# Moving three VectorE operations on a table ahead of two evacuations, in a Fourier-filter and feed-forward kernel

## The chip, the cores and the metric

One core of one Trainium2 chip. The metric is the device time of one execution in microseconds (us), the median of the runs of a kernel. Before the change it was 792.48 us (three runs, 791.69 to 793.87).

Names: TensorE is PE in the profile (its weight loads PEld), VectorE is DVE, ScalarE is ACT, GpSimd is POOL; SP only issues transfers. L291 is line 291 of the kernel's file. The change adds two lines above most of the code, so L443 of before is L445 of after.

## The reference, cut to what matters

```python
def _attn_ref(x, filt_r, filt_i):            # x: (8, 3008, 256), filters: (1505, 256)
    X = np.fft.rfft(x, axis=1)
    Y = X * (filt_r + 1j * filt_i)[None, :, :]
    return np.fft.irfft(Y, n=x.shape[1], axis=1)

def _moe_ref(x, w_in, w_out, beta):          # 24064 tokens, 256 -> 2048 -> 256
    h = x @ w_in
    return (h * (1.0 / (1.0 + np.exp(-beta * h)))) @ w_out
```

The kernel does the Fourier transforms as products with tables of sines and cosines, in two stages each way (3008 = 47 x 64). It makes the tables itself while the first of the eight batches is loading. From about 43 us on it is a steady stream of matmuls of the feed-forward part, with the later batches' filtering woven in.

## The kernel before

Only the set-up, the first 43 us, matters. The order in the source is the order of each engine's queue.

The angles of the second table are made in two halves of 12 x 64 columns: the first half on VectorE, the second on GpSimd.

```python
def angles(h, eng):
    ...
    eng.tensor_tensor(u[:], ka[...], kb[...], ALU.add)                     # L264
    eng.tensor_scalar(r[:], u[:], ROUND_C, ROUND_C, ALU.add, ALU.subtract) # L270: rounding
    eng.tensor_tensor(u[:], u[:], r[:], ALU.subtract)                      # L271
...
angles(0, nc.vector)
angles(1, gp)
```

ScalarE makes two of the table's five parts from the angles. The other three are a negated copy and two plain copies on VectorE:

```python
def t2_more(h, eng):
    ks_ = slice(h * NH, (h + 1) * NH)
    nc.vector.tensor_scalar_mul(t2[:, ks_, 4, :], t2[:, ks_, 1, :], -1.0)  # L290
    eng.tensor_copy(t2[:, ks_, 3, :], t2[:, ks_, 2, :])                    # L291
    eng.tensor_copy(t2[:, ks_, 0, :], t2[:, ks_, 1, :])                    # L292
```

The first stage of the first batch runs in eight units, each two PSUM tiles that are evacuated by VectorE (False) or ScalarE (True). `warm` puts dummy matmuls on TensorE.

```python
for i in range(2):
    first1(i, (True, True))
    warm(2 if i == 0 else 8)
t2_part(0, 0)                       # ScalarE
first1(2, (False, False))
warm(2)
for part in (1, 2):
    t2_part(0, part)                # ScalarE
...
for i in range(3, 5):
    first1(i, (False, False))
    warm(2)
t2_more(0, nc.vector)
first1(5, (True, True))
warm(2)
first1(6, (True, True))
warm(1)
first1(7, (False, True))
tabs = [table3(0, 0, ...), table3(0, 2, ...)]   # transposes of the table, L352
```

Then follow twelve products with the filter on VectorE, each two operations (L443). Products 1 to 3 read the first group of filter rows, 4 to 6 the second, 7 to 12 the third.

```python
for dst, ps in zip((p_t, q_t), pss):
    nc.vector.tensor_tensor(dst[:], ps[:], fri[:, 2 * i : 2 * i + 2, :], ALU.mult)
```

GpSimd's queue issues the loads of the feed-forward weights and of the second batch. They stand behind a small copy that reads the second filter group and so waits for it:

```python
for p0 in (H, M + H):
    gp.tensor_copy(held[p0 : p0 + H], fri[p0 : p0 + H, 2 * KG - 1, :1])
...
load_win(0)
load_win(1)
load_wout(0)
...                                  # second batch, the rest of the output weights
```

After the products: GpSimd scales the output weights as they land, SP's queue loads filter rows for the second batch, and one long VectorE operation ends the set-up.

```python
for i in range(4):
    scale_wout(i)                    # GpSimd, L149
for at in (0, M):
    for go in load_filter(frr, filt_r, at, 0, JG, nc.sync):
        go()
...
nc.vector.tensor_scalar_mul(t3[M:P], t3b[M:P], -1.0)      # L586, 64x3072
```

## Time and profile before

| before | us | view |
|---|---|---|
| span of the profiled execution | 789.8 | page |
| TensorE busy | 776.7 (98%) | page, part 1 |
| last table copy ends, table's transposes start | 16.52, 16.66 | timeline |
| first product, seventh product start | 18.89, 27.98 | timeline |
| last piece of the third filter group lands | 27.80 | times of landings |
| first product with the output weights (end of set-up) | 43.13 | timeline |

In a timeline line the columns are start, duration, engine, line, operation, out<-in, shape, count and, in brackets, idle time of the engine and what is thought to have ended it. This is VectorE's timeline before, 10 to 17 us:

```profile
10.58 2.88 DVE L107 CAST a_t<-psa 128x384 bf16<-128x384 f32 x6 [1.75 <-PE psa L326]
13.38 0.35 DVE L290 TENSOR_SCALAR t<-t 128x768 bf16<-128x768 bf16 x1
13.64 0.98 DVE L291 COPY t<-t 128x768 bf16<-128x768 bf16 x1
14.55 1.97 DVE L292 COPY t<-t 128x768 bf16<-128x768 bf16 x1
```

And GpSimd's, of the same time:

```profile
10.05 1.46 POOL L264 TENSOR_TENSOR u<-ka,kb 128x768 f32<-128x768 f32 x1
11.60 2.81 POOL L270 TENSOR_SCALAR r<-u 128x768 f32<-128x768 f32 x1
14.49 1.80 POOL L271 TENSOR_TENSOR u<-u,r 128x768 f32<-128x768 f32 x1
16.25 0.32 POOL L307 CAST id_f<-ident 16x16 f32<-16x16 bf16 x1
```

The three operations have the same shape. One took 0.35 us, one 0.98, one 1.97, and the two long ones end 0.2 us after a GpSimd operation: 14.41 and 16.29. TensorE waits for the last of them. The profile's bracket names another cause:

```profile
16.66 0.83 PE L352 MATMUL pt<-ident,t 128*128 128x128 bf16 x12 [2.28 <-POOL id_f L307]
```

The program waits there for VectorE's two table copies (the multiply stands ahead of them in the queue) and for an identity matrix that GpSimd had made by 5.7 us. GpSimd's L307 only happened to end at the same time. The wait of 2.28 us is VectorE's copy.

Further down, the seventh product and the long operation at the end of the set-up, with GpSimd's scaling beside it (VectorE's, VectorE's and GpSimd's timelines):

```profile
27.08 0.68 DVE L443 TENSOR_TENSOR qb_t<-ps2q,fri 128x512 bf16<-128x512 f32 x1
27.98 0.69 DVE L443 TENSOR_TENSOR pb_t<-ps,fri 128x512 bf16<-128x512 f32 x1 [0.22 <-PE pb L396]
```
```profile
40.66 1.49 DVE L586 TENSOR_SCALAR t<-t3b 64x3072 bf16<-64x3072 bf16 x1
```
```profile
39.44 1.89 POOL L149 TENSOR_TENSOR wout_sb<-frr,rbeta_sb 128x1024 bf16<-128x1024 f32 x1 [3.66 <-DMA frr<-in_moe_w_out_dram]
```

The seventh product idled 0.22 us and began 0.18 us after the last filter piece landed. That is the sign of a landing as the true cause, though the bracket says PE.

The DMA is nearly full all through the set-up. The view by stretches gives, for each, its length, the busy time and the instructions of PE, PEld, DVE, ACT and POOL, then the clock granted to TensorE, the DMA's busy share and its rate in GB/s:

```profile
17.00:28.00 11.00, 9.64 (x134) 8.65 (x132) 10.00 (x22) 10.13 (x18) 6.87 (x13) 1.00 1.08 221
28.00:36.30 8.30, 7.76 (x106) 6.73 (x104) 8.17 (x14) 6.77 (x13) 3.47 (x3) 1.00 1.06 252
```

### The profile page before, as it was taken

The numbers are of one execution on the slowest core, as the hardware profiler recorded it, in microseconds if no ns is written. First come the engines' busy times: TensorE is split into PE (matmuls) and PEld (weight loads), VectorE is DVE, ScalarE is ACT, GpSimd is POOL, SyncE is SP. The second block draws the span as 40 slices with busy tenths as digits, with TensorE's granted clock in tenths as the row PEclk, the third lists the DMA queues.
The fourth block names the chain that finished last, engine by engine and source line by source line (L and its number), as shares of the span: only waits on it lengthen the run. The fifth ranks groups of instructions, "written<-read, shape, count | busy, mean of one in ns | idle before, by whom it ended". The sixth has DMA issues, their size and how long they took to land.

```text
span 789.8 us, 15387 instructions
## 1 busy us (share of the span) xinstructions
PE 776.7 (98%) x6104; PEld 547.6 (69%) x6104; DVE 396.3 (50%) x644; ACT 596.9 (76%) x920; POOL 144.6 (18%) x143
## 2 busy tenths in 40 slices
PE   7899999999999999999999999999999999999998
PEld 4767667766777667876678766686667766776665
DVE  7946935755537464465534746367452761500101
ACT  5887886886678866788677876778767788677776
POOL 9322510330013200131002310024000340000000
PEclk9999999999999999999999999999999999999999
DMA  9978687116811178011860228412370214010101
GB/s 187 232 193 213 155 212 218 49 67 187 215 45 47 68 200 218 29 68 70 216 181 28 86 97 199 152 36 88 110 222 27 74 68 127 30 52 28 54 27 53
DMA packets 83380, 91.43 MB, mean 116 GB/s; under 512 B 3759, under 2 KB 73537, under 8 KB 82287
## 3 DMA queue, kind: packets, MB, share of 16 engines
q1 hardware_dynamic: 80204, 73.95, 30.5%
q0 software_dynamic: 2816, 16.26, 10.8%
q8 instruction: 47, 0.77, 0.4%
q10 hardware_dynamic: 288, 0.26, 0.1%
q14 instruction: 25, 0.20, 0.1%
HBM read 57.16 MB, written 46.66 MB: 131 GB/s over the span
## 4 chain that ended last, share of the span: by engine, by line
PE 93%; DVE 3%; POOL 2%; issue 1%; ACT 1%; DVEq 0%; ACTq 0%; POOLq 0%
PE acc L840 41%; PE hps L805 40%; PE ps L613 3%; PE ps L536 3%; PE ps L635 2%; PE ps L661 2%; DVE ost L107 1%; PE psz L456 1%; POOL xg L116 0%; POOL r L270 0%; ACT a L105 0%; DVE q_t L650 0%; DVE p_t L646 0%; DVE q_t L647 0%; PE pt L352 0%
## 5 line engine op out<-in xcount | busy, mean ns | idle before, releaser
L814 ACT ACTIVATE gT<-hps,beta_sb 128x512 bf16<-128x512 f32 x752 | 516.8, 687 | 175.3 <-PE hps L805 165.5
L840 PE MATMUL acc<-wout_sb,gT 128*128 128x256 bf16 x3008 | 455.1, 272 | 1.2 <-ACT ost L105 0.2
L805 PE MATMUL hps<-y,win_sb 128*128 128x512 bf16 (+7 forms) x1728 | 447.7, 351 | 0.3 <-DVE y L109 0.3
L840 PEld LDWEIGHTS <-gT 128*128 128x128 bf16 x3008 | 285.3, 98 | 132.7 <-issue 4.7
L805 PEld LDWEIGHTS <-win_sb 128*128 128x128 bf16 x1728 | 164.7, 98 | 24.8 <-issue 0.7
L651 POOL TENSOR_TENSOR v_t<-p_t,q_t 128x512 bf16<-128x512 f32 x84 | 106.7, 1270 | 375.3 <-DVE q_t L650 372.7
L107 DVE COPY ost<-acc 128x512 f32<-128x512 f32 (+1 forms) x88 | 56.2, 677 | 193.6 <-PE acc L840 188.0
L107 DVE CAST a<-ps 96x512 bf16<-96x512 f32 x96 | 65.9, 686 | 85.6 <-PE ps L613 85.6
L109 DVE TENSOR_SCALAR y<-ps 128x376 bf16<-128x376 f32 (+2 forms) x120 | 64.5, 541 | 64.3 <-PE ps L536 64.2
L646 DVE TENSOR_TENSOR p_t<-ps,frr 128x512 f32<-128x512 f32 x84 | 58.1, 691 | 31.8 <-PE ps L635 29.4
L650 DVE TENSOR_TENSOR q_t<-ps,fri 64x512 f32<-64x512 f32 x84 | 58.2, 693 | 1.2
L647 DVE SCALAR_TENSOR_TENSOR q_t<-ps,fri 64x512 f32<-64x512 f32 x84 | 57.4, 684 | 1.1
L536 PEld LDWEIGHTS <-zz 96*128 96x128 bf16 x512 | 35.4, 97 | 29.0
L105 ACT ACTIVATE z<-ps 128x512 bf16<-128x512 f32 x84 | 49.5, 590 | 0.7 <-PE ps L661 0.7
L613 PE MATMUL ps<-xg,t 94*96 94x512 bf16 x112 | 41.9, 381 | 0.2 <-DVE a L107 0.2
L536 PE MATMUL ps<-t,zz 96*128 96x94 bf16 x448 | 36.7, 204 | 0.0
L116 POOL DMA_DIRECT2D xg<-in_x_dram x22 | 12.1, 556 | 114.3 <-PE acc L840 97.7
L661 PE MATMUL ps<-v_t,t 128*128 128x256 bf16 x168 | 32.1, 273 | 0.4 <-DVE q_t L650 0.4
L635 PE MATMUL ps<-a,t 128*128 128x256 bf16 x168 | 32.1, 273 | 0.0
L635 PEld LDWEIGHTS <-t 128*128 128x128 bf16 x168 | 15.8, 98 | 14.6
L613 PEld LDWEIGHTS <-t 94*96 94x96 bf16 x112 | 13.8, 123 | 12.1
L661 PEld LDWEIGHTS <-t 128*128 128x128 bf16 x168 | 15.4, 98 | 8.1 <-DVE q_t L650 0.9
(119 smaller groups left out, 201.0 us busy)
## 6 DMA issues: line engine op xcount, KB each, us to landing
out_dram<-ost SPq DMA_DIRECT2D x40, 512.0 KB, 2.8
d<-a SPq DMA_DIRECT2D x28, 384.0 KB, 4.7
a<-d SPq DMA_DIRECT2D x28, 384.0 KB, 5.8
d<-z SPq DMA_DIRECT2D x28, 384.0 KB, 2.6
zz<-d SPq DMA_DIRECT2D x28, 384.0 KB, 4.8
xg<-in_x_dram POOLq DMA_DIRECT2D x6, 1280.0 KB, 10.2
frr<-in_filt_r_dram SPq DMA_DIRECT2D x12, 256.0 KB, 7.9
out_dram<-ost SPq DMA_DIRECT2D x22, 128.0 KB, 7.1
```

Source lines behind the costliest of these rows:

```text
L107: nc.vector.tensor_copy(dst, src)
L109: nc.vector.tensor_scalar_mul(dst, src, scale)
L536: nc.tensor.matmul(ps[:, e, :NP], lhsT=zz[:, jj + e, dc * P : (dc + 1) * P], rhs=tab[:], start=True, stop=True,)
L613: nc.tensor.matmul(ps[:KP], lhsT=t1[:], rhs=s["x"][:, 2 * i : 2 * i + 2, :], start=True, stop=True)
L635: nc.tensor.matmul(ps[:, e, :], lhsT=t2[:, k0 + e, 3:5, :].rearrange("p c k -> p (c k)"), rhs=s["a2"][g][:, kk + e, :], start=True, stop=True,
L646: nc.vector.tensor_tensor(p_t[:], ps[:], frr[:, ks_, :], ALU.mult)
L650: nc.vector.tensor_tensor(q_t[:M], ps[M:P], fri[M:P, ks_, :], ALU.mult)
L651: nc.gpsimd.tensor_tensor(v_t[:], p_t[:], q_t[:], ALU.add)
L661: nc.tensor.matmul(ps[:, e, :], lhsT=t3[:, k0 + e, :], rhs=v_t[:, e, :], start=True, stop=True)
L805: nc.tensor.matmul(hps[:, pos - t0 : pos - t0 + ln], lhsT=win_sb[:, dc, fb * P : (fb + 1) * P], rhs=ys[b][:, dc, n0 : n0 + ln], start=(dc ...
L814: nc.scalar.activation(gT[:, :tn], hps[:, :tn], ACT.Silu, scale=beta_sb[:, fb : fb + 1])
L840: nc.tensor.matmul(acc[tb // per][:, tb % per, :], lhsT=gT[:, tb * P : (tb + 1) * P], rhs=wout_sb[:, fb, :], start=(fb == 0 and tb % per = ...
```

## The change

Its intent: let the copies come before GpSimd's subtraction, so that they don't stand still behind it.

```diff
-    for i in range(3, 5):
-        first1(i, (False, False))
-        warm(2)
+    first1(3, (False, False))
+    warm(2)
+
     t2_more(0, nc.vector)
+    first1(4, (False, False))
+    warm(2)
     first1(5, (True, True))
```

(Units are counted from 0, as in the code: unit 4 is `first1(4, ...)`.) No instruction is added or removed. On VectorE the three table operations move ahead of the two evacuations of unit 4, which are 0.47 us each.

## The prediction

> **What bounds the kernel.** TensorE: 776.7 of a 789.8 us span (busy lines of the page), 93% of the chain that ended last, clock 1.0. The change touches only the first 17 us. The stretches of the set-up, 6 to 43 us, show DMA at its limit (busy share 1.0 or more), and several joints there wait for a landing.
>
> **What changes.** Nothing is added or removed. On VectorE three operations on the table (one multiply, two copies, 128x768 bf16) move ahead of unit 4's two evacuations. The timeline of VectorE before:
> - 10.58 to 13.46: six evacuations, one each 0.48 us
> - multiply at 13.38 (0.35 us); copy at 13.64 (0.98); copy at 14.55 (1.97)
> - the same three for the second half, at 24.16, GpSimd not computing: 0.35 us each, one every 0.27.
>
> The long ones end 0.2 us after a GpSimd operation: its rounding ends at 14.41, its subtraction (from 14.49) at 16.29. The Trainium skill ("SBUF — State Buffer", "SBUF: two separate sides") says VectorE's two-port modes and GpSimd exclude each other by a lock; the trace agrees for both copies (0.6 and 1.6 us lost), but not for the multiply, which ran inside the rounding at full speed. TensorE idles 2.3 us before the table's transposes (16.66); the wait is put down to a GpSimd copy, but what matters is VectorE's last copy (ends 16.52).
>
> After, the multiply starts near 12.5. Two branches:
> - (60%) all three run inside the rounding (11.6 to 14.41), or before the subtraction takes the lock: they end by 13.4 to 14.5, and the transposes start near 14.5 to 15, about 2 us earlier.
> - (40%) a copy is held to 14.41 and the last to 16.29, as now. Unit 4's evacuations come after 16.5, transposes start 0.5 us later, the first turn 0.9 us later.
>
> **How much is on the critical path.** Almost nothing, in either branch; later joints are fixed by DMA:
> 1. The first product needs the first filter group, landed at 17.09 (it now starts at 18.89): at most 1.7 us of the gain survives.
> 2. The seventh product needs the third filter group, whose last piece landed at 27.80. It started at 27.98 after 0.22 us of idle VectorE: already waiting for DMA. From there to 36.18 VectorE is gapless. So a gain of 2 us shrinks to about 0.05; a delay of 0.9 us by 0.2.
> 3. VectorE's 64x3072 multiply at 40.66 took 1.49 us, ending 0.8 us after GpSimd's scaling of output weights (39.44 to 41.33), which starts when they land (39.37). Started anywhere between 39.5 and 41.3 it ends at about 42.15. This absorbs a delay of up to 0.65 us.
>
> The weight transfers are issued behind a GpSimd copy that waits for a filter landing (18.27), so landings should hardly move.
>
> **Predicted time:** 792.4 us, range 791.4 to 793.6 (the three runs before spread over 2.2 us, more than the effect). Faster by over 2%: 0.005; within 2%: 0.99; slower: 0.005.
>
> **What the profile would show.** Right: the transposes start near 14.5 to 15; both copies shorter; the seventh product still at about 28.0, with VectorE's idle time before it grown from 0.2 to about 2 us; from 43 us on the traces coincide within 0.3 us. In the other branch the last copy still ends at 16.5 and the seventh product starts at about 28.5.
>
> **What would make it wrong.** The filter's last piece landing earlier, if GpSimd is held up and issues weight transfers later (some tenths gained); the delayed branch reaching the 64x3072 multiply later than 41.3; a changed meeting of that multiply with the scaling, worth up to 0.65 us. None is near 2%.

## More of the kernel before

The set-up ends here (TensorE's timeline):

```profile
43.13 0.38 PE L840 MATMUL acc<-wout_sb,gT 128*128 128x256 bf16 x2
```

## The result, and the profile after

After: 792.76 us median (six runs, 790.64 to 794.63); before, by then six runs, 792.33. Ratio 1.0003, 95% interval 0.9985 to 1.0021: the same. A ratio here is worked out from the fast runs of both kernels in the same rounds, so it is not quite the ratio of the medians.

VectorE's timeline of after, the lines that answer to those of before:

```profile
10.15 1.95 DVE L107 CAST a_t<-psa 128x384 bf16<-128x384 f32 x4 [1.33 <-PE psa L326]
12.02 0.62 DVE L290 TENSOR_SCALAR t<-t 128x768 bf16<-128x768 bf16 x1
12.57 0.35 DVE L291 COPY t<-t 128x768 bf16<-128x768 bf16 x1
12.84 0.35 DVE L292 COPY t<-t 128x768 bf16<-128x768 bf16 x1
...
24.60 0.68 DVE L445 TENSOR_TENSOR qb_t<-ps2q,fri 128x512 bf16<-128x512 f32 x1
27.92 0.69 DVE L445 TENSOR_TENSOR pb_t<-ps,fri 128x512 bf16<-128x512 f32 x1 [2.65 <-PE ps L436]
...
40.60 1.71 DVE L588 TENSOR_SCALAR t<-t3b 64x3072 bf16<-64x3072 bf16 x1
```

Both copies take 0.35 us. The transposes start 2.87 us earlier, at 13.79 (TensorE's timeline; no idle time stands before them). Not all of that is the change's: VectorE's evacuations began at 10.15 in this execution and at 10.58 in before's, since the first batch's third load had landed at 8.90 instead of 9.65.

```profile
13.79 0.83 PE L352 MATMUL pt<-ident,t 128*128 128x128 bf16 x12
```

The first product starts at 16.37, 2.5 us earlier. Then the lead is gone in one place: the seventh product starts at 27.92, only 0.06 us earlier than in before, after 2.65 us of idle VectorE. The bracket names TensorE, whose matmuls for it started at 26.07. The chain of waits of after has the filter transfer just ahead of that product, though it calls the idle time itself "issue", which means that the profile saw no cause (start, duration, what):

```profile
13.86 10.82 DMA fri<-in_filt_i_dram
24.68 0.60 DVE qb_t L445
25.28 2.55 issue
```

What decides is when that transfer landed: at 27.75 (27.80 in before), 0.17 us ahead of the product. From there on the two traces run alike. The first product with the output weights is at 43.30 in after and 43.13 in before, and the difference stays at 0.16 to 0.25 us to the end.

```profile
43.30 0.38 PE L842 MATMUL acc<-wout_sb,gT 128*128 128x256 bf16 x2
```

Where the 0.16 us come from: GpSimd's scaling began 0.16 us later in this execution, since its weights landed at 39.53 instead of 39.37, and VectorE's L588 ends behind it (39.60 + 1.90 = 41.50). This is GpSimd's line in after:

```profile
39.60 1.90 POOL L149 TENSOR_TENSOR wout_sb<-frr,rbeta_sb 128x1024 bf16<-128x1024 f32 x1 [4.08 <-DMA frr<-in_moe_w_out_dram]
```

### The profile page after: what moved, and what is told of

Read it like the earlier page. It is cut to its first block, busy times and chain, and to the rows that moved or that the text cites. A ratio compares the mean times of both kernels' runs of the same rounds, so it can differ in the third digit from the quotient of the medians.

```text
span 790.1 us, 15386 instructions
## 1 busy us (share of the span) xinstructions
PE 777.2 (98%) x6104; PEld 547.6 (69%) x6104; DVE 394.7 (50%) x644; ACT 597.1 (76%) x920; POOL 144.6 (18%) x143
## 4 chain that ended last, share of the span: by engine, by line
PE 92%; DVE 3%; DMA 3%; issue 2%; POOL 0%; ACT 0%; DVEq 0%; ACTq 0%; POOLq 0%
PE acc L842 41%; PE hps L807 40%; PE ps L615 3%; PE ps L538 3%; PE ps L637 2%; PE ps L663 2%; DMA fri<-in_filt_i_dram 1%; DVE ost L107 1%; DMA xg<-in_x_dram 1%; DMA mark<-xg 1%; DVE qb_t L445 0%; DVE pb_t L445 0%; DVE q_t L652 0%; DVE p_t L648 0%; DVE q_t L649 0%
## 5 line engine op out<-in xcount | busy, mean ns | idle before, releaser
L615 PEld LDWEIGHTS <-t 94*96 94x96 bf16 x112 | 13.8, 123 | 12.1
```

Source lines behind the costliest of these rows:

```text
L615: nc.tensor.matmul(ps[:KP], lhsT=t1[:], rhs=s["x"][:, 2 * i : 2 * i + 2, :], start=True, stop=True)
```

## The experiments

Theory: the change does save its 2 to 3 us, and the wait for the third filter group takes them back. Rivals: the lead is lost further down, where L588 meets the scaling; the filter's landing costs time by itself, whatever the order; or the order pays nothing and other transfers decide.

The marker for the end of the set-up is the start of the first product with the output weights. "Lead" is how much earlier something happens than in the profile of before.

### How long GpSimd's operation shuts VectorE out

The multiply of before ran inside GpSimd's rounding at full speed, and the copy behind it did not. So 96 short copies were run in a row beside GpSimd's three operations. They write into tables that are filled later, so results are right.

```diff
     t2_part(0, 0)
+    for n in range(96):
+        to = (t3b, t3)[n // 48].rearrange("p k c -> p (k c)")
+        nc.vector.tensor_copy(to[:, 64 * (n % 48) : 64 * (n % 48 + 1)], wz[:, :64])
     first1(2, (False, False))
```

> Before, with 96 short copies (128x64 bf16, into tables that are written later, results right) run one behind the other on VectorE from about 9 us on, across GpSimd's addition, rounding and subtraction for the second half's angles; time does not matter here. Theory A (GpSimd's operation takes the shared port only while it reads and while it writes, with a free stretch between): inside the rounding (11.6 to 14.4) copies stand still for about 0.7 us at its start and 0.7 us at its end and pass at their usual rate, under 0.1 us each, in between; inside the subtraction (1.8 us) they stand still all through. Theory B (the port is held for the whole operation, and the multiply that ran inside the rounding was an accident of its start): one copy stands still for all of each GpSimd operation, 1.4, 2.8 and 1.8 us. Theory C (it is given back in pieces): many short stops all through the rounding, and GpSimd's rounding gets longer than 2.81 us.

One run, 800.95 us, correct. GpSimd's timeline of this kernel:

```profile
10.36 1.46 POOL L264 TENSOR_TENSOR u<-ka,kb 128x768 f32<-128x768 f32 x1
11.91 2.84 POOL L270 TENSOR_SCALAR r<-u 128x768 f32<-128x768 f32 x1
14.83 1.86 POOL L271 TENSOR_TENSOR u<-u,r 128x768 f32<-128x768 f32 x1
```

VectorE's timeline of it, in four narrow windows (inside the addition, at the start of the rounding, at its end, inside the subtraction):

```profile
10.39 1.48 DVE L345 COPY t3b<-wz 128x64 bf16<-128x64 bf16 x1
...
11.96 0.81 DVE L345 COPY t3b<-wz 128x64 bf16<-128x64 bf16 x1
...
13.88 0.99 DVE L345 COPY t3b<-wz 128x64 bf16<-128x64 bf16 x6
...
14.93 1.79 DVE L345 COPY t3b<-wz 128x64 bf16<-128x64 bf16 x1
```

An undisturbed copy takes 0.17 us and one starts every 0.086 us. One copy stood still for nearly all of the addition, and one for nearly all of the subtraction. In the rounding one stood still from 11.96 to 12.77. Then 15 passed at the usual rate. Then five that began from 13.97 on all ended between 14.79 and 14.87. So the rounding shuts VectorE out for about 0.65 us at its start and 0.75 us at its end, and leaves it alone for about 1.3 us between. That is theory A. B fails, and C fails (two stops, not many, and the rounding kept its 2.8 us). Why the rounding takes the port like this, reading first and writing last, is the theory's wording; the run shows only the two stops.

The other traces hold a second sign of the stop at the end, and it shows that GpSimd waits as well. In four executions a table operation on VectorE was still running 2.13 us after the rounding had begun. In each the rounding ended 0.68 us after that operation, and took 2.84 to 2.97 us instead of 2.81. GpSimd's scaling, too, took 2.19 us instead of 1.89 where VectorE's long operation had begun before it (the second kernel with wrong filter rows, below).

This explains before: the multiply at 13.38 fell into the free stretch, the first copy ran into the end of the rounding, and the second came to VectorE (14.55) just after the subtraction had begun (14.49). It also explains the 0.62 us of the multiply in after: it came to VectorE at 12.02, in the first stop.

### Only the multiply moves

```diff
+    nc.vector.tensor_scalar_mul(t2[:, :NH, 4, :], t2[:, :NH, 1, :], -1.0)
     first1(4, (False, False))
     warm(2)
     ...                              # the two copies stay behind unit 4
```

> Part of the change: only the table's multiply moves ahead of unit 4's evacuations, the two copies stay behind them. Theory (the port is free in the middle of GpSimd's rounding, about 12.3 to 13.7, and held at its end and all through the subtraction): the multiply takes 0.35 to 0.65 us near 12.0 to 12.5; the first copy comes to VectorE near 13.5, passes in 0.35 us or is held to 14.4; the second is held to the end of the subtraction, 16.3 to 16.6; the transposes start near 16.6 as in before. Rival (what counts is to come before the subtraction is issued, at 14.5): both copies end before 14.6 and the transposes start before 15.2.

One run, 792.38 us, correct. VectorE's and GpSimd's timelines of this kernel:

```profile
10.04 1.95 DVE L107 CAST a_t<-psa 128x384 bf16<-128x384 f32 x4 [1.21 <-PE psa L327]
11.91 0.74 DVE L374 TENSOR_SCALAR t<-t 128x768 bf16<-128x768 bf16 x1
12.57 1.01 DVE L107 CAST a_t<-psa 128x384 bf16<-128x384 f32 x2
13.50 0.34 DVE L292 COPY t<-t 128x768 bf16<-128x768 bf16 x1
13.77 0.97 DVE L293 COPY t<-t 128x768 bf16<-128x768 bf16 x1
```
```profile
11.61 2.91 POOL L270 TENSOR_SCALAR r<-u 128x768 f32<-128x768 f32 x1
14.61 1.82 POOL L271 TENSOR_TENSOR u<-u,r 128x768 f32<-128x768 f32 x1
```

The first copy passed, as expected. The second was held only to the end of the rounding, not to the end of the subtraction, and the transposes started at 14.79. Here the rival's numbers were nearer. The operation that stands waiting when the rounding ends goes through first; only one that comes behind it meets the subtraction. In before the first copy took that place, and the second met the subtraction. The run does not show that moving the multiply alone helps: its copies stand behind the same six evacuations and the multiply as in before. They came earlier because the evacuations began at 10.04 instead of 10.58, the input's third load having landed at 7.91 instead of 9.65.

### Taking the filter's landing away

Products 7 to 12 of the first batch read rows of the first two groups, which have landed. All transfers stay as they are. Done in both orders, in the same rounds. Their outputs are wrong, which doesn't matter for the times.

```diff
-            nc.vector.tensor_tensor(dst[:], ps[:], fri[:, 2 * i : 2 * i + 2, :], ALU.mult)
+            f0 = 2 * (i % 6)
+            nc.vector.tensor_tensor(dst[:], ps[:], fri[:, f0 : f0 + 2, :], ALU.mult)
```

In the order of before:

> The order of before, wrong on purpose: products 7 to 12 of the first batch read filter rows of the first two groups, so that VectorE waits for no landing of the third group. Theory (the gain of the change is lost in the wait for the third filter group, landed at 27.8 us): this kernel hardly had that wait, 0.2 us, so the seventh product starts at about 27.75 instead of 27.98, and the first product with the output weights still at about 43.1; time ratio to before 1.000. Rival (the third group's landing is a cost by itself, in both orders): this one too starts the seventh product over 1 us earlier and ratio is below 0.998.

793.33 us median (six runs) against 793.49 (eleven runs of before); ratio 0.9996, interval 0.9977 to 1.0016. Its profile cannot be laid beside that of before: TensorE was granted half its clock from 18.0 to 21.4 us in that execution. This is the stretch, and the 3.4 us before it (view by stretches; the third number from the end is the clock):

```profile
14.58:18.00 3.42, 1.19 (x22) 1.22 (x23) 3.13 (x5) 0.84 (x4) 3.18 (x5) 1.00 1.15 268
18.00:21.41 3.41, 3.26 (x25) 2.61 (x23) 2.53 (x6) 2.42 (x4) 3.29 (x8) 0.50 0.95 209
```

In the order of after:

> The same wrong filter rows, in the order of after. Theory: with the wait for the third group gone, the seventh product starts at about 25.2 us (27.92 in after), and the lead of 2.7 us lasts to the end of the set-up: VectorE's 64x3072 multiply begins near 37.9, before the second scaling of output weights (39.5), and takes 0.85 instead of 1.71 us; the first product with the output weights starts near 40.0 to 40.4 instead of 43.30; time about 789.3 us, ratio to before 0.996. Rival (the lead is lost further down, in the meeting of the multiply with the scaling or in transfers of weights and input): the seventh product starts earlier but the first product with the output weights not before 42.5, ratio 0.999 to 1.001.

790.94 us median (six runs); ratio 0.9975, interval 0.9957 to 0.9994. VectorE's timeline of this kernel:

```profile
25.05 0.68 DVE L446 TENSOR_TENSOR pb_t<-ps,fri 128x512 bf16<-128x512 f32 x1
...
37.72 0.96 DVE L589 TENSOR_SCALAR t<-t3b 64x3072 bf16<-64x3072 bf16 x1
```

The seventh product starts at 25.05 without idle time. L589 comes before the scaling and takes 0.96 us. The first product with the output weights starts at 39.82, a lead of 3.3 us, even a little more than expected. So the same order that gains nothing in after gains about 2 us once the wait for the landing is gone, and the order of before gains nothing from it. The rivals of both runs fail. The time gained is less than the expected ratio of 0.996, and part of it comes with TensorE's clock (see the open ends below). In the profile the lead shrank later, from 3.3 us at 43 us to 1.9 us at the end; 0.9 us of it went at 131 us, where TensorE waited for a read of an intermediate result.

### Letting the filter land earlier, with right results

The copy that holds back GpSimd's queue reads the third group's first two pieces instead of the second group, so that the weights share the DMA with less of the filter.

```diff
-    for p0 in (H, M + H):
-        gp.tensor_copy(held[p0 : p0 + H], fri[p0 : p0 + H, 2 * KG - 1, :1])
+    for p0 in (0, M):
+        gp.tensor_copy(held[p0 : p0 + H], fri[p0 : p0 + H, 4 * KG - 1, :1])
```

In the order of after:

> After, right results, with the weight and input transfers of GpSimd's queue held until the third group's first two pieces have landed (before: until the second group's). Theory: the third group's last piece no longer shares the DMA with the weights and lands near 26.3 instead of 27.75; the seventh product starts there, 26.4; the multiply of 64x3072 begins near 39.1, before the scaling, and takes 0.85 us; the first product with the output weights starts near 41.4 instead of 43.30; ratio to before about 0.9975. Rival (transfers are only put off: weights land later and something waits for them instead): the seventh product starts near 26.4 but the first product with the output weights is not earlier than 42.8, ratio 1.000 or above.

791.02 us median, ratio 0.9974, interval 0.9955 to 0.9992, correct. The filter landed at 26.0, the seventh product started at 26.18, L588 took 0.96 us, and the set-up's marker came at 40.96. So far as the theory had it. But in this profile most of the lead was lost at 53.8 us (the longest of TensorE's waits from 43 to 80 us: who waited for whom, total us, times, longest):

```profile
PE ps L538 <- DVE a L107: 1.4, 1, 1.4
```

VectorE had waited 4.5 us there for the landing of a store that stood behind filter loads in SP's queue. So the rival was right in kind: something else waits next. The profiled execution, the slowest of the six (792.89 us), lost the rest of its lead at 134 us and ended 0.2 us behind that of before. So the gain stands in the mean of the runs alone; this profile does not show it to the end.

In the order of before, in other rounds:

> The order of before with the same hold of GpSimd's queue as the held kernel of after, right results. Theory (hold and change pay only together): the third filter group lands near 26.0, but VectorE reaches the seventh product only at about 27.7, so that product starts 0.2 to 0.3 us earlier than before's 27.98, the 64x3072 multiply again meets the scaling of output weights and takes about 1.5 us, the first product with the output weights starts at 42.9 to 43.3; ratio to before 0.999 to 1.001. Rival (the hold alone is the gain, whatever the order): ratio near 0.9975, like after with the hold.

792.33 us median, ratio 0.9997, interval 0.9983 to 1.0011, correct. The time is as the theory had it, the profile not: in that execution the table's copies had passed at 13.25 and 13.52, the seventh product started at 25.70 and the marker came at 40.48 (VectorE's timeline):

```profile
13.25 0.35 DVE L291 COPY t<-t 128x768 bf16<-128x768 bf16 x1
13.52 0.35 DVE L292 COPY t<-t 128x768 bf16<-128x768 bf16 x1
```

The first batch's third and fourth loads had landed at 8.98 and 9.69 us, in before's profile at 9.65 and 10.08. So before's order is not always held: whether it is depends on when the input lands. One profile of before had not shown that.

The changed kernel beside it, again:

> The changed kernel again, on the chip and in the rounds of the others. Theory: ratio to before 0.999 to 1.001; transposes of the table near 13.8, seventh product near 27.9 with over 2 us of idle VectorE before it. Rival (the change gains a little that six runs could not show): ratio 0.998 or below.

792.30 us median, ratio 1.0002, interval 0.9984 to 1.0020. Transposes at 14.47, the seventh product at 28.36 after 1.98 us of idle VectorE, the marker at 43.13. As the theory had it.

Both held kernels were run once more, now in the same rounds:

> The held kernel in the order of after, once more on another chip and in the same rounds as the one of before. Theory (the change pays once the third filter group lands earlier): ratio to before 0.997 to 0.9985. Rival (the 0.9974 of the first time was scatter, for its profile had lost the lead again by 60 us): ratio 0.999 to 1.001.

> The held kernel in the order of before, once more. Its first profile had the copies pass within the rounding, since the input had landed 0.6 us sooner than in before's profile. Theory: where the last copy comes to VectorE after about 13.8 us it is held to the end of the subtraction and the seventh product starts near 27.7; where it comes sooner all pass and the product starts at the filter's landing, near 26; so the mean lies between before and the held after: ratio 0.998 to 1.0005. Rival (order plays no part in the held kernel): the same ratio as the held after within 0.0005.

Order of after: 791.55 us, 0.9986 (0.9972 to 1.0000). Order of before: 792.02 us, 0.9996 (0.9982 to 1.0010). Both within what the theory said, but the gain of the held after is half of the first time's. In the profile of the second, the last copy (0.97 us, from 13.69) was held to the end of the rounding only, although the theory had set the limit at 13.8. Both profiles reached the marker together, at 41.57 and 41.55. So for the held kernel the rival, that order plays no part, is not excluded: the two intervals overlap.

### Moving the next joint too

First try: the four filter loads of the second batch go to the end, behind the stores.

```diff
-    for at in (0, M):
-        for go in load_filter(frr, filt_r, at, 0, JG, nc.sync):
-            go()
...
-            for k0 in range(JG, NK, JG)
+            for k0 in range(0, NK, JG)
```

> After with the hold, and with the first four loads of the second batch's filter moved behind the stores of its first stage (to where the other loads of it are issued), right results. In the held kernel's profile VectorE waited 4.5 us for the first of those stores to land (52.9) and TensorE lost 1.44 us at 53.8, two thirds of the lead. Theory: with the filter loads out of the way the stores land before 50, that wait goes, and the lead of 2.2 us at the first product with the output weights (41.0) is still there at 60 us; ratio to before 0.9965 to 0.998. Rival (the DMA is full up to 48 us whatever the order, and the store lands no earlier than 52): lead at 60 us is again about 0.6 us; ratio 0.999.

793.22 us, ratio 1.0005 (0.9991 to 1.0019), correct: a miss. The store landed at 47.4 and the lead was still 2.5 us at 60 us, as expected. But now the loads landed at 66 to 70 us, too late for the second batch's first product (VectorE's waits, 60 to 72 us):

```profile
DVE p_t L644 <- DMA frr<-in_filt_r_dram: 5.2, 1, 5.2
DVE y L109 <- PE ps L534: 3.7, 2, 2.2
```

At 79 us this kernel was 1.3 us behind before. Second try: the loads stand between the second and the third store. In both orders, in the rounds of the two repeated runs above.

```diff
             nc.sync.dma_start(s["d1r"][:, g * JG : (g + 1) * JG, :], s["a1"][:])
+            if b == 1 and g == 1:
+                for at in (0, M):
+                    for go in load_filter(frr, filt_r, at, 0, JG, nc.sync):
+                        go()
```

> After with the hold, and the first four loads of the second batch's filter issued between the second and the third store of its first stage: later than in after, earlier than in the kernel that had them last and waited 5.2 us for them at 70 us. Right results. Theory: the first store lands near 47.5 (no wait at 54), the filter loads land by 55 (no wait at 70), and the lead of over 2 us is there at 60 and at 80 us; a wait for a read at 134 us, seen in several profiles of both orders, may take some of it; ratio to before 0.9965 to 0.998. Rival (some other transfer becomes the next joint): lead at 80 us under 1 us, ratio over 0.9985.

789.69 us median (five runs, 789.50 to 790.32), ratio 0.9967, interval 0.9954 to 0.9979, correct. It beats both kernels, by 0.33% of before. The store landed at 47.3, the loads by 54.1, and TensorE's waits from 43 to 80 us are down to one line:

```profile
PE pz L526 <- DVE q_t L652: 0.3, 1, 0.3
```

The marker came at 40.90; the lead of 2.2 us was still whole at 130 us and 1.7 us at the end.

> The same two moves of transfers in the order of before. Theory: as with the hold alone, between before and the kernel beside it, depending on where the copies fall: if they are held, first product with the output weights near 42.5 to 43 and lead under 0.5 us; if not, as the kernel beside it; ratio 0.9975 to 1.000, and not below the one beside it. Rival (transfers alone are the gain): the same ratio as the kernel beside it within 0.0005.

791.76 us median (five runs, 790.06 to 792.87), ratio 0.9990, interval 0.9976 to 1.0004, correct. Its profile can't show the cause, for it had both luck and bad luck: the copies passed, but TensorE's clock was at half from 35.7 to 39.1, so that L586 met the scaling (1.58 us) and the marker came at 42.92.

| transfers | order of before | order of after |
|---|---|---|
| as they were | 1 | 1.0003, 1.0002 |
| no wait for the third group (wrong results) | 0.9996 | 0.9975 |
| held | 0.9997, 0.9996 | 0.9974, 0.9986 |
| held, loads between the stores | 0.9990 | 0.9967 |

All are ratios to before. In the three cases run in the same rounds in both orders, the mean of the order of after over that of before's is 0.9979, 0.9991 and 0.9976 (from the runs' means: 791.20 over 792.85, 791.43 over 792.11, 789.78 over 791.64). No interval was made for these. No row of the order of before clears 1 by its interval; of the order of after all three lower rows do or touch it.

## Why the prediction was right

It said 792.4 us, between 791.4 and 793.6; it came to 792.76. The number alone proves little, since the range is about as wide as the scatter of before's own runs, and a change without effect would most likely have hit it. What tests the prediction are its steps.

- **The copies were held by GpSimd, and moving them frees them.** Shown: both copies take 0.35 us in both profiles of after, and in all seven profiles of its order; in the order of before they do so in two of five (see the last point). The prediction left open why the multiply got through; the row of short copies showed the free stretch in the rounding. It had given this branch 60%.
- **The transposes about 2 us earlier, near 14.5 to 15.** They came at 13.79 and 14.47, in the two profiles of after. The input also lands at different times: four evacuations began at 10.15 and 10.84.
- **At most 1.7 us of the gain survive at the first product.** Too small in one profile of after: 2.5 us, since the first filter group landed at 16.19 in that execution, not at 17.09. In the other it landed at 17.16 and the product came 1.56 us earlier than in before. The prediction treated one execution's landing as fixed. It did not matter.
- **The seventh product stays at about 28.0, with idle VectorE before it grown to about 2 us.** Shown: 27.92 with 2.65 us, 28.36 with 1.98 us. Taking that wait away lets the order of after gain 0.25%.
- **The long operation ends 0.8 us after the scaling, wherever it starts beside it.** Shown: it ended 0.8 us after the scaling in before and in both profiles of after, though it began at 40.66, 40.60 and 41.03. This was a smaller joint: once the lead passes it, it takes 0.96 us.
- **Not seen:** that before itself is sometimes not held. Five executions of its copy order were profiled. Where the evacuations began at 9.83 and 10.19 us, both copies passed; at 10.35 one was held to the end of the rounding; at 10.58 (before) and 10.75 both were held. In after's order all passed, with starts from 9.75 to 10.84. So the 2.3 us were not in each execution to be gained, and that the copies were held in the one profile the prediction had was in part chance.

What stays open: how much of the order's 0.1 to 0.25%, once the wait was moved or removed, comes from held copies, and how much from TensorE's clock. Apart from the kernel with the short copies, two profiles were disturbed, each with half the clock for 3.4 us. Both were in before's order; none of seven in after's order was. The record says more, for it has each run's mean clock, and both disturbed profiles read 0.998. In the order of before 24 of the 53 runs with a clock on record read 0.998 or less, in that of after 5 of 40. That is hardly chance, but no run shows what in the order does it. Only the runs at a clock of 1.000, few as they are, compare the orders without it:

| runs at clock 1.000, mean us (runs) | order of before | order of after | difference here; in all runs |
|---|---|---|---|
| no wait for the third group | 791.92 (2) | 790.73 (4) | 1.2; 1.7 |
| held | 791.59 (2) | 791.32 (4) | 0.3; 0.7 |
| held, loads between the stores | 791.46 (2) | 789.78 (5) | 1.7; 1.9 |

So part of the gain goes with the clock, least where both transfers were moved. And the held kernel in before's order had a lead of 2.7 us at 43 us in one profile, 1.4 us at its end, yet no gain on the mean of its runs; landings and clock differ from run to run by as much as this effect.

## What to carry to other kernels

Before taking a wait away, ask of the next few joints down the queue whether they wait for this engine or for a transfer that nothing here moves: an idle time of 0.2 us that ends just after a landing means that any lead stops there. A saved stall is then not lost, but it pays only together with an earlier landing, and each landing put earlier makes another later, so the next joint has to be read again after each move. And one profile shows one set of landing times; a stall that depends on them should be looked for in a second one.

## What the Trainium skill lacked or had wrong

- "SBUF — State Buffer", "Who interferes with whom": it says that whichever of a VectorE operation in a two-port mode and a GpSimd operation issues first "gets the shared pair for the whole instruction". The runs agree for GpSimd's operations of two tensors (one copy took 1.79 us instead of 0.17 beside a subtraction of 1.86 us) and differ for the rounding with two scalars: of its 2.84 us VectorE was shut out for about 0.65 us at the start and 0.75 us at the end, and 15 copies passed between.
- The same section lacks what happens between two GpSimd operations 0.08 us apart: a VectorE operation already waiting went first (0.97 us, ended at 14.74 with the subtraction issued at 14.61), one that came 0.06 us after the subtraction's start waited for all of it (1.97 us).
- "GPSIMD Engine Reference", "4.1 Engine selection": it calls one-input elementwise operations "roughly line-rate". The rounding, one input and two scalar steps on 768 fp32 elements, took 2.81 us, longer than the addition (1.46) and the subtraction (1.80) of two inputs of that shape.
- "TensorE: Matmul & The Clock Gate", "What's actually happening": it has the clock halved after an idle window of about 3.4 us. The kernel with the short copies agrees: TensorE was idle from 12.0 us, and the clock was at half from 16.4. In the two other profiles the half-clock stretches had that length (3.41 us), but TensorE was not idle in the stretches of the same length before them: it was busy for 1.19 us in the first (transposes only) and for 2.09 us in the second (mostly other matmuls).
